# A scratch tensor stored by pairs of classes, read back into spread partitions on one queue

## The chip, the cores and the metric

The kernel runs on one core of a Trainium2 chip. A core has five engines with queues of their own: TensorE (PE, matrix products), VectorE (DVE), ScalarE (ACT), GpSimd (POOL) and SyncE (SP), which here only issues DMAs. SyncE's DMAs go through the queue that the profile calls q1 (hardware_dynamic), GpSimd's through q0 (software_dynamic). Both feed the same 16 DMA engines.

The metric is the time of one execution on the device, in microseconds (us). The kernel before takes 406.85 us, the median of three runs from 404.64 to 407.57. The profile comes from one more execution.

## The reference

Two layers follow each other. Here `x` is 8 x 5696 x 128 and `h` is 5696 x 128.

```python
Yf = np.fft.rfft(x, n=2*S, axis=1) * np.fft.rfft(h, n=2*S, axis=0)[None]   # long convolution
x  = np.fft.irfft(Yf, n=2*S, axis=1)[:, :S, :]
X  = np.fft.rfft(x, axis=1)                     # spectral mixing, first 64 modes only
Y[:, :64] = einsum('bmd,mde->bme', X[:, :64], w_r + 1j*w_i)
u  = x + np.fft.irfft(Y, n=S, axis=1)
out = u + np.maximum(u @ w_ch, 0.0)
```

## The kernel before

The sequence of 5696 positions is written as 89 x 64. A Fourier step over the 89 gives 90 frequency *classes* (`NK`), and the step over the 64 (`J`) is done class by class. The batch of 8 is taken in four groups of two (`NP` = 4, index `g_`). Every operation is recorded by a small planner, the `Recorder`, which derives each wait from named tokens that an operation reads, writes or must come after. Engines run their lists in the order of recording. The diff lies in three places, and the order of the work around them is this.

**Ticks.** A group runs through 23 ticks (`tick`, `NT` = 23) of up to four classes. A tick's matmuls transform four classes of both batch elements. VectorE multiplies with the spectrum of `h` (`products`, tensors U, Hs), two more matmuls per element turn the result back over the 64 positions, and ScalarE writes it in float16 to a small ring of buffers (Zs and Zt, lines 569 to 571). Such a buffer holds, on 128 partitions (real and imaginary part of 64 positions), four classes of 2 x 128 values. SyncE writes it to the scratch tensor `zscr` in DRAM (line 573): class after class, in each 128 rows of 256 values, so that every packet has 512 B. The same buffers feed matmuls that collect the 64 modes for the second layer. While the fourth group runs, GpSimd loads what comes later, in the table `early` by tick: the weights W, the table S4 in two parts (`load_s4`), and at tick 21 the first blocks of Z. The first block waits for the Z writes of ticks 0 to 14 of that group (`SLACK`).

**The passage.** After the last tick come 128 short matmuls of the modes with W, the transposes of their result Y, and in between the first work of the output stage (`u_z` with `alone`).

**Output stage.** It needs Z the other way round: for a position p within the 64, all classes on partitions. A *block* is one group's Z for 16 positions (`ZB`), 16 blocks in all. `load_zt` reads a block into one of five tiles: 180 rows (90 classes, real and imaginary), 8 KB each, the first 128 rows in part a on partitions 0 to 127, the other 52 in part b on partitions 32 to 83. Partitions 0 to 31 of part b are set to zero by GpSimd (line 477), since the matmul with part b covers partitions 0 to 83. Blocks 0 to 4 are read by GpSimd, the other 11 by SyncE, which also writes the output. A block's tile is loaded again when the block is used up: line 762, for the block five places on. `u_tile` makes 8 positions of one batch element: one matmul that adds the second layer (`u_c`, tables IBs, C), and for each position two matmuls with 89 columns, parts a and b of the block against parts a and b of S4. ScalarE or VectorE writes the result to UT. `o_tile` multiplies UT with `w_ch` and the identity (WI), ScalarE takes the ReLU into R, VectorE adds into O, and SyncE writes 512 KB for every pair of them. In group 0 only `u_tile` runs; from group 1 on the `o_tile`s of the group before are mixed in.

The reads of blocks 0 to 4 are recorded with two calls in `early` and two behind the ticks:

```python
NT - 2: lambda: (load_zt(0, "gpsimd", SLACK), load_ib(), load_zt(1, "gpsimd"), load_zt(2, "gpsimd"))}
...
load_wi()
load_zt(3, "gpsimd")
load_zt(4, "gpsimd")
```

All these tiles lie over tensors of the earlier stages. `zt_old` names the tokens whose readers must be done before a tile is first written; for block 4 they are the tables M and G.

Of the kernel before, what the change touches and what calls it, by code (L numbers as in the profile page):

```python
# [4 lines left out]
P = 128  # L5
F16 = mybir.dt.float16
# [117 lines left out]
def bass_long_conv_fft__then__afno_spectral_mix_kernel(nc, x, h, moe_w_r, moe_w_i, moe_w_ch, out):  # L124
# [31 lines left out]
    pos = J * qq[None, :] + pp[:, None]  # L156
    ang = 2.0 * np.pi * kk[:, None, None] * pos[None] / L
    s4 = np.stack([back[:, None, None] * np.cos(ang), -back[:, None, None] * np.sin(ang)], axis=0)
    RB, PB = 2 * NK - P, 32
    rows = s4.transpose(1, 0, 2, 3).reshape(2 * NK, S)  # L160
    s4t = np.zeros((P, 2 * S))
    s4t[:, 0:S] = rows[0:P]
    s4t[PB:PB + RB, S:2 * S] = rows[P:2 * NK]
    tt = np.arange(S)
    am = 2.0 * np.pi * np.outer(tt, np.arange(M)) / S
    modes = np.concatenate([np.cos(am), -np.sin(am)], axis=1)
# [75 lines left out]
    xt = at("XT", B * XTW, F16, a_g + GW * 2 + 2048 * (NZX - NZ))  # L242
    assert GW * 2 + 2048 * (NZX - NZ) + B * XTW * 2 <= HW * 2

    ZB = 16
    NC = 5
    ZP = ZB * 2 * D
    a_h2, a_xt = a_h + HW * 2, a_x + 4 * S + 2 * B * P
    a_as1, a_m2 = a_as + 2 * S, a_m + 4 * S
    zt_off = [(a_h, a_h2), (a_as1, a_as1 + 2 * ZP), (a_h + 2 * ZP, a_h2 + 2 * ZP), (a_as1 + 4 * ZP, a_as1 + 6 * ZP),  # L250
              (a_m2, a_g)]
    assert 2 * S + 8 * ZP <= AW * 2
    zt = [[at(f"ZT{i}{'ab'[p_]}", ZP, F16, zt_off[i][p_]) for p_ in range(2)] for i in range(NC)]
    ib_sb = at("IBs", S, F16, a_m)
    s4_sb = [at("S4a", S, F16, a_m + 2 * S), at("S4b", S, F16, a_as)]
    assert 4 * S + 2 * ZP + 4 * P + 2048 <= 2 * MW
    wi_sb = at("WI", 2 * P, F16, a_m2 + 2 * ZP)
    u_off = [a_x, a_x + 2 * S, a_st, a_st + 2 * S]
    u_sb = [at(f"UT{i}", S, F16, u_off[i]) for i in range(4)]
    o_big = [a_h + 4 * ZP, a_h2 + 4 * ZP, a_st + 4 * S] + [a_g + 2 * ZP + 4096 * i for i in range(2)] + \  # L260
            [a_xt + 4096 * i for i in range(2)]
    o_off = [a_h + 4 * ZP + 4096, a_h2 + 4 * ZP + 4096, a_m2 + 2 * ZP + 4 * P]
    NO8, NO = len(o_big), len(o_off)
# [18 lines left out]
        return bass.AP(ps, p0 * 4096 + bank * 512 + off, [[4096, n]] + [list(d) for d in dims])  # L282

    R = Recorder(nc)
    for name, n in (("c", 16), ("x", 26), ("z", 8), ("w", 16), ("t", 10), ("s", 8), ("o", 12), ("p", 16), ("q", 10)):
        R.ring(name, n)

    def bank(i):
# [175 lines left out]
    WT = [("w", i) for i in range(4)]  # L464
    ZY = [("zs", i, b) for i in range(NZL, NZX) for b in range(2)]
    ZX = [("zs", i, b) for i in range(NZ, NZL) for b in range(2)]
    zt_old = [(H_ALL, H_ALL), (AST, AST), (H_ALL, H_ALL), (AST, AST), (M_ALL[3:6], G_ALL)]

    def load_zt(i, eng="sync", more=()):
        g_, c_ = divmod(i, J // ZB)  # L470
        for part, (p0, r0, n) in enumerate(((0, 0, P), (PB, P, RB))):
            old = once(("zt", i % NC, part), zt_old[i % NC][part])
            if more:
                old = list(old) + list(more)
            if old and part:
                z32 = zt[i][1][0:PB, :].bitcast(U32)
                R.add("gpsimd", lambda e: e.memset(z32, 0), (), [("zt0", i)], after=old)  # L477
            dma(eng, bass.AP(zt[i % NC][part], p0 * ZP, [[ZP, n], [1, ZP]]),
                bass.AP(zs, (g_ * 2 * NK + r0) * J * 256 + c_ * ZB * 256, [[J * 256, n], [1, ZP]]),
                "q" if eng == "gpsimd" else "t", [("zd", g_, s_) for s_ in range(NT)], [("zt", i % NC, part)], after=old)  # L480

    def load_ib():
        dma("gpsimd", ib_sb[:, :], c_ib.ap(), "p", (), [("ib",)], after=M_ALL[0:2] + pace)

    def load_s4(part):
        n = PB + RB if part else P
        dma("gpsimd", s4_sb[part][0:n, :], bass.AP(c_s4, part * S, [[2 * S, n], [1, S]]), "p", (),
            [("s4", part)], after=pace + (AST if part else M_ALL[1:4]))

    V, A = "vector", "scalar"  # L490
    border = {NT - 1: [(0, 2, V)], NT: [(1, 0, V), (2, 2, A)], NT + 1: [(3, 0, V), (4, 2, A)], NT + 2: [(5, 0, V), (6, 2, V)]}
    early = {0: lambda: load_id(), 1: lambda: load_w(0), 3: lambda: load_w(1), 6: lambda: load_w(2), 8: lambda: load_w(3),
             12: lambda: load_s4(1), 16: lambda: load_s4(0),
             NT - 2: lambda: (load_zt(0, "gpsimd", SLACK), load_ib(), load_zt(1, "gpsimd"), load_zt(2, "gpsimd"))}
# [42 lines left out]
    def tick(g_, t):  # L537
        if g_ + 1 < NP:
            for i in range(2 * XC):
                if t == XPLACE[g_ > 0][i]:  # L540
                    x_place(i, x_st[i], xtok(i))
        with_h = with_h_at(g_, t)
        if t < NT:
            sl = XSLOT[0] if with_h else XSLOT[(t + (g_ == 0)) % 2]
            for i, k in enumerate(ticks[t]):
                for r in range(2):
                    for b in range(2):
                        col = k * 3 * J + (J if r == 0 else 0) + b * J
                        mm(pv(sl + b, i * D, [[1, D]]),
                           ap(m_sb, MW, J * b, J, col, [[1, P]]),  # L550
                           ap(a_sb, AW, J * b, J, (2 * k + r) * D, [[1, D]]), r == 0, r == 1,
                           AST + mtok(k), [bank(sl + b)])
            products(g_, t, sl)
        if t in border and g_ + 1 < NP:
            for j, sl, e in border[t]:
                a_tile(j, [sl], e)
        if g_ + 1 < NP and t % 2 == 0 and 0 < t <= 4 * XC:
            i = t // 2 - 1
            x_load(g_ + 1, i, x_st[i], xtok(i), [("u", t % NU)] + AST)
        if LC <= t < NT + LC:  # L560
# [12 lines left out]
            dma("sync", bass.AP(zs, zo, [[256, P], [P * 256, n], [1, 256]]),  # L573
                bass.AP(z_s[zi], 0, [[1024, P], [256, n], [1, 256]]), "z",
                [("zs", zi, 0), ("zs", zi, 1)], [("zd", g_, s_)])
        if LM <= t < NT + LM:
            s_ = t - LM
            zi = s_ % NZS[g_]
            if s_ == 0:
                mm(pv(MB, 0, [[1, 2 * P]]), m_sb[ZR:P, 0:P], ap(f1_sb, 2 * NK, ZR, P - ZR, 0, [[0, 2], [1, P]]), True, False, [("f1",)] + mtok(0), [bank(MB)])  # L580
            for i, k in enumerate(ticks[s_]):
                for b in range(2):
                    if k % 2:
                        o, off, n, sl = pv(MB, b * P, [[1, P]]), (k + 1) // 2 * P, P, (k + 1) // 2
                    else:
                        ms, off = even[k]
                        n, sl = 2 * len(ms), 0
                        dims = [[M, 2]] if len(ms) == 1 else [[ms[1] - ms[0], 2], [M, 2]]
                        o = pv(MB, b * P + ms[0], dims)
                    mm(o, z_s[zi][:, i * 256 + b * P:i * 256 + b * P + P], g_sb[:, off:off + n],  # L590
                       False, k == NK - 1 and b == 1, [("g", sl // GP), ("zs", zi, b)], [bank(MB)])
        if with_h:
            filter_tick(t + LH, [2, 3])
# [26 lines left out]
                    dma("gpsimd", dst, src_, ring, (), [tok], after=[("as", j)])  # L620


    load_wi()
    load_zt(3, "gpsimd")
    load_zt(4, "gpsimd")

    LSLOT = [4, 6, 0, 2]
    NCH = J // ZB
# [3 lines left out]
    def u_z(i, b, half, alone=False):  # L632
        g_, c_ = divmod(i, NCH)
        t = turns("l", LSLOT)
        z = zt[i % NC]
        for hb in range(2):
            if alone:
                mm(pv(t + hb, 0, [[1, 4 * NQ]]), f1_sb[ZR:P, 0:P], ap(f1_sb, 2 * NK, ZR, P - ZR, 0, [[0, 2], [1, 2 * NQ]]),
                   True, False, [("f1",)], [bank(t + hb)])
            else:  # L640
                u_c(i, b, half, t, hb, True)
            for pl in range(4):
                for ri in range(2):
                    pz = half * 8 + hb * 4 + pl
                    so = (c_ * ZB + pz) * NQ
                    n = (P, PB + RB)[ri]
                    mm(pv(t + hb, pl * NQ, [[1, NQ]]), z[ri][0:n, pz * 256 + b * P:pz * 256 + b * P + P], s4_sb[ri][0:n, so:so + NQ],
                       False, not alone and pl == 3 and ri == 1, [("zt", i % NC, ri), ("zt0", i % NC), ("s4", ri)], [bank(t + hb)])
        if alone:
            ahead[(i, b, half)] = t  # L650
        return t
# [149 lines left out]
```

## Time and profile before

| | |
|---|---|
| three runs | 407.57, 406.85, 404.64 us |
| the profiled execution | 409.74 us, of which its span is 407.7 us |
| mean granted clock of TensorE | 0.977 of full speed |
| TensorE busy | 376.7 us, 92% of the span |
| VectorE / ScalarE busy | 311.8 us (76%) / 296.4 us (73%) |
| GpSimd busy | 81.4 us (20%) |
| ticks of group 3 | about 229 to 272 us |
| passage | 272 to 291 us |
| output stage | 291 to 407.7 us |
| SyncE's queue (q1) | 62379 packets, 67.73 MB, 48.1% of the time of 16 engines |
| GpSimd's queue (q0) | 24288 packets, 37.31 MB, 43.0% |
| Z writes (zscr from Zs and Zt) | 88 of 256 KB and 4 of 128 KB |
| last Z write, 128 KB | 15.8 us from issue to landing |

Tensors go by the program's names: ZT0a is part a of the tile that holds blocks 0, 5, 10 and 15, ZT4b is part b of the tile of blocks 4, 9 and 14. The helper lines 312 (matmul), 300 and 302 (ScalarE), 304 and 306 (VectorE) and 309 (DMA) stand for many places, so rows are told apart by their tensors. A chain is followed back from the last instruction: at each step to what released it. In a table of waits, the first name is the one that waited.

### The profile page before, as it was taken

Reading aid. Unit: us, or ns where it says so; the run is one execution under the profiler, and the core shown is the slowest. Engines: PE = TensorE matmul, PEld = TensorE weight load, DVE = VectorE, ACT = ScalarE, POOL = GpSimd, SP = SyncE. Lnnn points to the kernel's source line nnn. Section 1 sums busy time; section 2 is a strip of 40 time slices with the busy share of each in tenths; the row PEclk is TensorE's granted clock in tenths of the full one; section 3 lists DMA queues with packets and bytes.
Section 4 is the critical chain, followed back from the end, with each engine's and each line's share of the span. In section 5 each row is a group of like instructions: output and inputs, shape, how many; then the busy total and the mean of one; then the engine's idle time right before and its main releaser. Section 6 shows DMA issues by size and latency. Waiting matters only on the chain.

```text
span 407.7 us, 12527 instructions
## 1 busy us (share of the span) xinstructions
PE 376.7 (92%) x5398; PEld 286.7 (70%) x5398; DVE 311.8 (76%) x341; ACT 296.4 (73%) x477; POOL 81.4 (20%) x133
## 2 busy tenths in 40 slices
PE   7979899998999988899989899997978999999994
PEld 7978666656756657656658666665767889888873
DVE  6878789997899997889997888850324677777876
ACT  1458599987978977788878888960434777777775
POOL 8300022210823202723304011039100000000000
PEclk9999999999999999999999999995798999999999
DMA  8997379995989993989985499999998999999869
GB/s 159 194 320 271 101 162 280 274 278 159 138 137 218 251 233 80 141 154 207 245 224 95 48 311 346 285 274 394 417 390 340 314 350 420 406 419 390 347 251 357
DMA packets 86720, 105.81 MB, mean 260 GB/s; under 512 B 22494, under 2 KB 72286, under 8 KB 82846
## 3 DMA queue, kind: packets, MB, share of 16 engines
q1 hardware_dynamic: 62379, 67.73, 48.1%
q0 software_dynamic: 24288, 37.31, 43.0%
q8 instruction: 42, 0.69, 0.7%
q14 instruction: 11, 0.09, 0.1%
HBM read 72.49 MB, written 51.12 MB: 303 GB/s over the span
## 4 chain that ended last, share of the span: by engine, by line
PE 56%; DMA 14%; DVE 11%; ACT 9%; POOL 6%; issue 2%; SPq 0%; DVEq 0%; POOLq 0%
PE ps L312 56%; DVE U L528 5%; DMA ZT4b<-zscr 5%; DVE As L306 5%; DMA Xr<-in_x_dram 4%; ACT As L302 4%; DMA zscr<-Zt 3%; POOL Xr L309 2%; DMA Hs<-Hs 2%; ACT Xs L300 2%; ACT R L735 1%; ACT UT L300 1%; ACT Zt L300 1%; DVE Xin L348 1%; POOL ZT1b L477 0%
## 5 line engine op out<-in xcount | busy, mean ns | idle before, releaser
L528 DVE TENSOR_TENSOR U<-Xs,Hs 128x2048 f16<-128x2048 f16 x70 | 82.7, 1190 | 20.2 <-ACT Xs L300 20.0
L312 PE MATMUL ps<-U,Wc 128*128 128x512 f16 (+1 forms) x368 | 93.6, 377 | 1.9 <-DVE U L528 1.9
L300 ACT CAST Zs<-ps 128x512 f16<-128x512 f32 (+1 forms) x142 | 75.7, 592 | 9.4 <-PE ps L312 9.4
L300 ACT CAST Xs<-ps 128x1024 f16<-128x1024 f32 x70 | 69.4, 996 | 15.6 <-PE ps L312 14.6
L736 DVE TENSOR_TENSOR O<-ps,R 128x512 f32<-128x512 f32 x81 | 52.5, 685 | 20.4 <-ACT R L735 12.0
L735 ACT ACTIVATE R<-ps 128x512 f32<-128x512 f32 x96 | 50.9, 572 | 18.8 <-PE ps L312 18.4
L306 DVE TENSOR_SCALAR As<-ps 128x720 f16<-128x720 f32 x68 | 57.6, 900 | 9.1 <-PE ps L312 8.5
L312 PE MATMUL ps<-As,M 64*128 64x128 f16 x1440 | 55.8, 217 | 5.1 <-ACT Xs L300 2.0
L312 PE MATMUL ps<-F,Xin 128*128 128x180 f16 x512 | 53.5, 249 | 7.0 <-DVE As L306 2.8
L312 PEld LDWEIGHTS ps<-F,Xin 128*128 128x128 f16 x512 | 44.6, 155 | 14.5 <-DVE As L306 4.1
L302 ACT ACTIVATE As<-ps 128x720 f16<-128x720 f32 x60 | 46.3, 785 | 10.6 <-PE ps L312 9.7
L312 PE MATMUL ps<-WI,UT 128*128 128x256 f16 x360 | 52.3, 280 | 0.5 <-DVE O L736 0.4
L312 PEld LDWEIGHTS ps<-As,M 64*128 64x128 f16 x1440 | 40.7, 94 | 15.1 <-DVE U L528 3.2
L312 PEld LDWEIGHTS ps<-U,Wc 128*128 128x128 f16 x368 | 29.1, 98 | 31.6 <-DVE U L528 2.4
L528 DVE TENSOR_TENSOR U<-ps,Hs 128x2048 f16<-128x2048 f32 x22 | 50.2, 2283 | 0.8 <-DMA Hs<-Hs 0.8
L309 POOL DMA_DIRECT2D Xt<-in_x_dram x48 | 25.5, 536 | 109.7 <-PE ps L312 94.7
L300 ACT CAST UT<-ps 128x712 f16<-128x712 f32 x40 | 30.0, 752 | 20.7 <-PE ps L312 19.7
L312 PEld LDWEIGHTS ps<-WI,UT 128*128 128x128 f16 x360 | 39.4, 152 | 4.3 <-issue 1.9
L312 PE MATMUL ps<-IBs,C 128*128 128x356 f16 x128 | 40.6, 327 | 0.6
L312 PEld LDWEIGHTS ps<-G,Zs 128*128 128x128 f16 x556 | 28.1, 96 | 14.9
L304 DVE CAST UT<-ps 128x712 f16<-128x712 f32 x24 | 21.4, 891 | 17.0 <-PE ps L312 17.0
L312 PE MATMUL ps<-G,Zs 128*128 128x128 f16 (+2 forms) x556 | 34.3, 192 | 0.0
(84 smaller groups left out, 497.0 us busy)
## 6 DMA issues: line engine op xcount, KB each, us to landing
out_dram<-O SPq DMA_DIRECT2D x39, 512.0 KB, 8.3
zscr<-Zs SPq DMA_DIRECT2D x68, 256.0 KB, 6.2
Xt<-in_x_dram POOLq DMA_DIRECT2D x24, 320.0 KB, 6.9
zscr<-Zt SPq DMA_DIRECT2D x20, 256.0 KB, 6.9
W<-wscr POOLq DMA_DIRECT2D x4, 1024.0 KB, 8.5
M<-cM POOLq DMA_DIRECT2D x5, 720.0 KB, 20.4
ZT0a<-zscr SPq DMA_DIRECT2D x3, 1024.0 KB, 9.9
Hs<-Hs SPq DMA_DIRECT2D x44, 64.0 KB, 5.9
```

What stands on the lines that cost most here:

```text
L300: R.add(e, lambda h_: h_.copy(dst, src), reads, writes, after=after)
L302: R.add(e, lambda h_: h_.activation(dst, src, COPY, scale=scale), reads, writes, after=after)
L304: R.add(e, lambda h_: h_.tensor_copy(dst, src), reads, writes, after=after)
L306: R.add(e, lambda h_: h_.tensor_scalar_mul(dst, src, scale), reads, writes, after=after)
L309: R.add(eng, lambda h_: h_.dma_start(dst, src), reads, writes, ring=ring, after=after)
L312: R.add("tensor", lambda h_: h_.matmul(o, l, r, start=st, stop=sp), reads, writes)
L348: R.add("vector", lambda e: e.tensor_copy(bass.AP(x_sb, i * XN * XS, [[XW, NQ], [XS, XN], [1, D]]), bass.AP(src, 0, [[XB, NQ], [D, XN], [1 ...
L528: R.add("vector", lambda e: e.tensor_tensor(uv, src, hv, MULT), bk + [("h", t, 0), ("h", t, 1, 0), ("h", t, 1, J)], [("u", i)])
L735: R.add("scalar", lambda e: e.activation(rv, src_r, RELU), bk, [("r", i % NR)], after=once(("r", i % NR), G_ALL + XTT + [("y", 0), ("y", 1 ...
L736: R.add("vector", lambda e: e.tensor_tensor(ov, src_u, rv, ADD), bk + [("r", i % NR)], [key + (h_,)], after=once(key, old))
```

## The change

Three things are done.

1. **Z's scratch by pairs of classes.** Row p of two neighbouring classes is stored together, 512 values. A buffer of four classes is written as two pairs, with packets of 1 KB.
2. **A block's rows spread.** The real and imaginary part of a pair of classes are two rows of 16 KB in a block, 90 rows in all. Rows 0 to 63 go to the even partitions 0, 2, ... 126, rows 64 to 89 to partitions 1, 5, ... 101. The other 38 partitions are set to zero, once for each tile, by a memset of the whole tile before its first read (`clear_zt`). The two matmuls for a position now take the first and the second class of every pair, each over 128 partitions. The table S4 is laid out in the same way, with a memset of its own for each part.
3. **GpSimd issues all reads of Z.** The two DMAs of each of the 16 blocks are on GpSimd's queue. SyncE has only the output in that stage.

With this the tiles move: a block has one tile of 16 KB a partition in place of two parts of 8 KB. Tile 4 now lies at the start of G, which covers the first of the buffers Zt too, so its memset also comes after the readers of those (`G_ALL + ZX + ZY`); two output buffers change place. The memsets of tiles 1 and 0 are at ticks 14 and 17 of the last group, those of the others right ahead of their reads.

```diff
-    s4t[:, 0:S] = rows[0:P]
-    s4t[PB:PB + RB, S:2 * S] = rows[P:2 * NK]
+    s4t = s4.transpose(1, 0, 2, 3).reshape(NK // 2, 2, 2, S).transpose(0, 2, 1, 3).reshape(NK, 2 * S)
...
+    SPREAD = ((0, J, 0, 2), (J, NK - J, 1, 4))
...
-    zt_off = [(a_h, a_h2), (a_as1, a_as1 + 2 * ZP), (a_h + 2 * ZP, a_h2 + 2 * ZP), (a_as1 + 4 * ZP, a_as1 + 6 * ZP),
-              (a_m2, a_g)]
+    zt_off = [a_h, a_as1, a_h2, a_as1 + 4 * ZP, a_g]
...
-    zt_old = [(H_ALL, H_ALL), (AST, AST), (H_ALL, H_ALL), (AST, AST), (M_ALL[3:6], G_ALL)]
-
-    def load_zt(i, eng="sync", more=()):
+    zt_old = [H_ALL, AST, H_ALL, AST, G_ALL + ZX + ZY]
+
+    def load_zt(i, more=()):
         g_, c_ = divmod(i, J // ZB)
-        for part, (p0, r0, n) in enumerate(((0, 0, P), (PB, P, RB))):
...
+        old = list(once(("zt", i % NC), zt_old[i % NC])) + list(more)
+        for part, (r0, n, p0, st) in enumerate(SPREAD):
+            dma("gpsimd", bass.AP(zt[i % NC], p0 * 2 * ZP, [[st * 2 * ZP, n], [1, 2 * ZP]]),
+                bass.AP(zs, g_ * NK * P * 256 + r0 * J * 512 + c_ * ZB * 512, [[J * 512, n], [1, 2 * ZP]]),
+                "q", [("zd", g_, s_) for s_ in range(NT)] + [("zc", i % NC)], [("zt", i % NC, part)], after=old)
+
+    def clear_zt(i):
+        z32 = zt[i][:, :].bitcast(U32)
+        R.add("gpsimd", lambda e: e.memset(z32, 0), (), [("zc", i)], after=list(zt_old[i]) + pace)
...
     def load_s4(part):
...
+        s32 = s4_sb[part][:, :].bitcast(U32)
+        R.add("gpsimd", lambda e: e.memset(s32, 0), (), [("s4z", part)], after=old)
+        for h_, (r0, n, p0, st) in enumerate(SPREAD):
...
-             NT - 2: lambda: (load_zt(0, "gpsimd", SLACK), load_ib(), load_zt(1, "gpsimd"), load_zt(2, "gpsimd"))}
+             14: lambda: clear_zt(1),
+             17: lambda: clear_zt(0),
+             NT - 2: lambda: (load_zt(0, SLACK), load_ib(), load_zt(1), clear_zt(2), load_zt(2))}
...
-            dma("sync", bass.AP(zs, zo, [[256, P], [P * 256, n], [1, 256]]),
-                bass.AP(z_s[zi], 0, [[1024, P], [256, n], [1, 256]]), "z",
+            dma("sync", bass.AP(zs, zo, [[512, P], [P * 512, n // 2], [1, 512]]),
+                bass.AP(z_s[zi], 0, [[1024, P], [512, n // 2], [1, 512]]), "z",
...
     load_wi()
-    load_zt(3, "gpsimd")
-    load_zt(4, "gpsimd")
+    clear_zt(3)
+    load_zt(3)
+    clear_zt(4)
+    load_zt(4)
...
-                    mm(pv(t + hb, pl * NQ, [[1, NQ]]), z[ri][0:n, pz * 256 + b * P:pz * 256 + b * P + P], s4_sb[ri][0:n, so:so + NQ],
+                    zo = pz * 512 + ri * 256 + b * P
+                    mm(pv(t + hb, pl * NQ, [[1, NQ]]), z[:, zo:zo + P], s4_sb[ri][:, so:so + NQ],
```

More of the change, by code (lines that the diff above doesn't have):

```diff
@@ L158, in bass_long_conv_fft__then__afno_spectral_mix_kernel @@
     s4 = np.stack([back[:, None, None] * np.cos(ang), -back[:, None, None] * np.sin(ang)], axis=0)
-    RB, PB = 2 * NK - P, 32
-    rows = s4.transpose(1, 0, 2, 3).reshape(2 * NK, S)
-    s4t = np.zeros((P, 2 * S))
-    s4t[:, 0:S] = rows[0:P]
-    s4t[PB:PB + RB, S:2 * S] = rows[P:2 * NK]
+    s4t = s4.transpose(1, 0, 2, 3).reshape(NK // 2, 2, 2, S).transpose(0, 2, 1, 3).reshape(NK, 2 * S)
     tt = np.arange(S)
@@ L249, in bass_long_conv_fft__then__afno_spectral_mix_kernel @@
     a_as1, a_m2 = a_as + 2 * S, a_m + 4 * S
-    zt_off = [(a_h, a_h2), (a_as1, a_as1 + 2 * ZP), (a_h + 2 * ZP, a_h2 + 2 * ZP), (a_as1 + 4 * ZP, a_as1 + 6 * ZP),
-              (a_m2, a_g)]
+    zt_off = [a_h, a_as1, a_h2, a_as1 + 4 * ZP, a_g]
     assert 2 * S + 8 * ZP <= AW * 2
-    zt = [[at(f"ZT{i}{'ab'[p_]}", ZP, F16, zt_off[i][p_]) for p_ in range(2)] for i in range(NC)]
+    zt = [at(f"ZT{i}", 2 * ZP, F16, zt_off[i]) for i in range(NC)]
     ib_sb = at("IBs", S, F16, a_m)
@@ L259, in bass_long_conv_fft__then__afno_spectral_mix_kernel @@
     u_sb = [at(f"UT{i}", S, F16, u_off[i]) for i in range(4)]
-    o_big = [a_h + 4 * ZP, a_h2 + 4 * ZP, a_st + 4 * S] + [a_g + 2 * ZP + 4096 * i for i in range(2)] + \
+    o_big = [a_h + 4 * ZP, a_h2 + 4 * ZP, a_st + 4 * S] + [a_m2 + 4096 * i for i in range(2)] + \
             [a_xt + 4096 * i for i in range(2)]
@@ L284, in bass_long_conv_fft__then__afno_spectral_mix_kernel @@
     R = Recorder(nc)
-    for name, n in (("c", 16), ("x", 26), ("z", 8), ("w", 16), ("t", 10), ("s", 8), ("o", 12), ("p", 16), ("q", 10)):
+    for name, n in (("c", 16), ("x", 26), ("z", 8), ("w", 16), ("t", 10), ("s", 8), ("o", 12), ("p", 16), ("q", 12)):
         R.ring(name, n)
@@ L466, in bass_long_conv_fft__then__afno_spectral_mix_kernel @@
     ZX = [("zs", i, b) for i in range(NZ, NZL) for b in range(2)]
-    zt_old = [(H_ALL, H_ALL), (AST, AST), (H_ALL, H_ALL), (AST, AST), (M_ALL[3:6], G_ALL)]
-    def load_zt(i, eng="sync", more=()):
+    zt_old = [H_ALL, AST, H_ALL, AST, G_ALL + ZX + ZY]
+    def load_zt(i, more=()):
         g_, c_ = divmod(i, J // ZB)
-        for part, (p0, r0, n) in enumerate(((0, 0, P), (PB, P, RB))):
[L472 to L480, printed above, removed]
+        old = list(once(("zt", i % NC), zt_old[i % NC])) + list(more)
[6 more added lines that the diff above has]
+        R.add("gpsimd", lambda e: e.memset(z32, 0), (), [("zc", i)], after=list(zt_old[i]) + pace)
     def load_ib():
@@ L485, in load_s4 @@
     def load_s4(part):
-        n = PB + RB if part else P
-        dma("gpsimd", s4_sb[part][0:n, :], bass.AP(c_s4, part * S, [[2 * S, n], [1, S]]), "p", (),
-            [("s4", part)], after=pace + (AST if part else M_ALL[1:4]))
+        old = pace + (AST if part else M_ALL[1:4])
+        s32 = s4_sb[part][:, :].bitcast(U32)
+        R.add("gpsimd", lambda e: e.memset(s32, 0), (), [("s4z", part)], after=old)
+        for h_, (r0, n, p0, st) in enumerate(SPREAD):
+            dma("gpsimd", bass.AP(s4_sb[part], p0 * S, [[st * S, n], [1, S]]), bass.AP(c_s4, (r0 * 2 + part) * S, [[2 * S, n], [1, S]]),
+                "p", [("s4z", part)], [("s4", part, 0, h_)], after=old)
     V, A = "vector", "scalar"
@@ L620, in bass_long_conv_fft__then__afno_spectral_mix_kernel @@
                     dma("gpsimd", dst, src_, ring, (), [tok], after=[("as", j)])
+    pace[:] = []
     load_wi()
-    load_zt(3, "gpsimd")
-    load_zt(4, "gpsimd")
+    clear_zt(3)
+    load_zt(3)
+    clear_zt(4)
+    load_zt(4)
     LSLOT = [4, 6, 0, 2]
@@ L645, in u_z @@
                     so = (c_ * ZB + pz) * NQ
-                    n = (P, PB + RB)[ri]
-                    mm(pv(t + hb, pl * NQ, [[1, NQ]]), z[ri][0:n, pz * 256 + b * P:pz * 256 + b * P + P], s4_sb[ri][0:n, so:so + NQ],
-                       False, not alone and pl == 3 and ri == 1, [("zt", i % NC, ri), ("zt0", i % NC), ("s4", ri)], [bank(t + hb)])
+                    zo = pz * 512 + ri * 256 + b * P
+                    mm(pv(t + hb, pl * NQ, [[1, NQ]]), z[:, zo:zo + P], s4_sb[ri][:, so:so + NQ],
+                       False, not alone and pl == 3 and ri == 1, [("zc", i % NC), ("zt", i % NC, 0), ("zt", i % NC, 1), ("s4", ri, 0, 0), ("s4", ri, 0, 1), ("s4z", ri)], [bank(t + hb)])
         if alone:
@@ L700, in bass_long_conv_fft__then__afno_spectral_mix_kernel @@
     o_cur = [0]
-    o8_old = [H_ALL] * 2 + [U_ALL] + [G_ALL + ZX] * 2 + [WT] * 2
+    o8_old = [H_ALL] * 2 + [U_ALL] + [M_ALL[3:6]] * 2 + [WT] * 2
     o_old = [H_ALL] * 2 + [M_ALL[5:6]]
```

## The prediction

> **What bounds the kernel now.** I read the chain of work that ended last, then who waited for whom on TensorE, then the granted clock in steps of 1 us, then the DMA queues in windows. After the loads at the start the chain is nearly all engine work, and TensorE is busy 100% of the time from 240 to 270 us and 99% from 320 to 380. The exception is the passage from the ticks to the output stage (start, duration, work):
>
> ```profile
> 260.02 10.88 DMA zscr<-Zt
> ...
> 271.95 1.81 POOL ZT0b L477
> ...
> 284.73 1.74 POOL ZT4b L477
> 286.47 20.44 DMA ZT4b<-zscr
> 306.91 0.04 issue
> 306.95 13.93 PE ps L312 x182
> ```
>
> A write of Z, landed at 270.9, releases GpSimd's first read of Z. Five blocks follow with a memset in each, and the last part of the fifth takes 20.4 us to land. TensorE's waits there (total, times, longest):
>
> ```profile
> PE ps L312 <- DMA ZT4b<-zscr: 2.4, 1, 2.4
> PE ps L312 <- DMA ZT0b<-zscr: 2.4, 1, 2.4
> PE ps L312 <- DMA ZT3b<-zscr: 0.7, 1, 0.7
> PE ps L312 <- DMA ZT4a<-zscr: 0.7, 1, 0.7
> ```
>
> That is 6.2 us of plain waiting. The clock adds to it (last three columns: granted clock, DMA share, GB/s):
>
> ```profile
> 276.00:277.00 1.00, 1.00 (x40) 1.00 (x37) 0.29 (x1) 0.00 (x0) 1.00 (x1) 0.55 0.83 287
> 289.00:290.00 1.00, 1.00 (x9) 0.62 (x8) 0.53 (x1) 0.78 (x2) 0.00 (x0) 0.63 0.99 418
> 306.00:307.00 1.00, 0.05 (x1) 0.05 (x2) 0.00 (x0) 0.00 (x0) 0.00 (x0) 0.91 0.96 401
> 310.00:311.00 1.00, 1.00 (x17) 0.93 (x15) 0.69 (x1) 0.18 (x2) 0.00 (x0) 0.89 0.79 336
> ```
>
> Between the first two rows the clock is 0.50, and again between the last two: about 276.55 to 289.63 and 306.91 to 310.11. The first drop comes before any wait for Z, under the 128 short matmuls on W, so it will stay.
>
> Why do blocks 3 and 4 come late? In the window 280 to 284 GpSimd's queue moves 1.66 MB in 4 us, 415 GB/s, with the engines to itself. In 300 to 306, while TensorE waits for block 4 on that queue, SyncE's queue has taken the engines:
>
> ```profile
> q0 software_dynamic: 182, 1.66, 97.6%
> ...
> q1 hardware_dynamic: 250, 1.75, 71.7%
> q0 software_dynamic: 98, 0.60, 23.7%
> ```
>
> (packets, MB, share; first row 280 to 284, the others 300 to 306). SyncE issues the reads of blocks 5, 6 and 7, not needed before 310, at 290.8, 294.7 and 298.7, and they pass block 4.
>
> **The change, part by part.**
>
> *Reads all on GpSimd.* Blocks 0 to 4 and the two small tables are 5 x 1.475 + 1.458 + 0.066 = 8.9 MB; with about 1 MB of Z writes still outstanding at 271.4 that is 9.9 MB. The rows of GB/s sum to 9.0 MB by 295 and 9.9 MB by 297; what landed until 306.9 was 13.7 MB, so 3.8 MB of later blocks had gone ahead. In one queue they can't. Block by block at the measured 410 GB/s: block 1 lands at about 285, block 2 at 289, block 3 at 293.
>
> Block 4 has a condition of its own. Its tile now lies over two of the buffers from which Z is written, so its memset waits for the very last Z write. That one was issued at 273.0 and took 15.8 us, so 288.8. The memset is 128x4096 words; the nearest row is
>
> ```profile
> L477 POOL MEMSET ZT0b<- x1: 1824/1824/1824, 271.9 to 271.9; 32x2048 uint32 x1
> ```
>
> so 0.89 ns a word and 3.65 us, if the number of partitions doesn't count. The block's reads are issued at 292.5 and 293.0 and land 6.7 to 7.1 us later by the rows of block 0: 299.6. TensorE needs it after blocks 1 to 3 at 3.93 us each (290.80, 294.7, 298.7 in the SyncE reads they release): from block 1 at 289.5 (below) that is 301.3. All three late waits go, 3.8 us, and with them the half-speed 3.2 us that follow: 1.6 us. **5.4 us.**
>
> *Block 0.* GpSimd's memset between its two parts goes, so the second part is issued 0.53 us behind the first, not 2.3. Lower bound of the first issue: VectorE's product of tick 21 ends at 269.9; upper: 271.4 as now. With 7 us to land, block 0 is there between 277.5 and 279; I take 278.3 against 280.84, 2.5 us earlier. TensorE then runs at half clock until 289.63, so 2.5 us are worth half: **1.3 us**, block 1 starting at 289.5. If the clock came back one of its steps of 3.4 us earlier it would be 1.6 us more; that is an end of the range.
>
> *GpSimd's added work before the passage.* Two memsets of 2848 words (2.53 us each) and two of 4096 (3.65 each), two more DMA issues (0.53). From 253.5: 2.53 + 1.07 + 3.65 ends at 260.7; from 260.9 the same again ends at 268.2. The earliest start of block 0 is 269.9, so 1.7 us of idle GpSimd hide it: zero. VectorE's operations that ran beside a memset kept their time (the 128x512 cast of Y, inside the memset at 275.3, took 0.69 us; the 712-wide cast alone takes 0.90), but none of these has two inputs in SBUF as the products have. Bounds: zero to all 12.4 us added to VectorE; I take zero, the nearest row. [...]
>
> *Z written by pairs.* 22,528 fewer packets. In 276 to 280 SyncE's queue spends 48.2% of 64 engine-us on 1159 packets of 512 B, 26.6 ns each; at the rate of the long rows 512 B would take 19.3. So 7.3 ns a packet, some 10 us of all 16 engines over the span, 2.5 of it in the last group. TensorE is busy throughout there; the one wait that it could end is VectorE's 0.8 us for a mirrored half of H. Zero to 0.8; I take zero.
>
> *Matmuls.* Same number; 128 rows for 84 costs nothing (204 and 203 ns in the rows of ZT0b and ZT0a).
>
> *What is late next.* The DMA engines. From 271.4: 5 us for tables and last Z writes, 23.6 MB of Z at 424 GB/s = 55.7, 23.3 MB of output at 406 GB/s (the window 366 to 376) = 57.4. That ends at 389.5 at the earliest, against a last matmul at 399.4 - 6.7 = 392.7. It still fits: zero, with up to 2 us of waiting for output buffers as the bound.
>
> **Sum:** 5.4 + 1.3 = 6.7 us off the profiled execution's span of 407.7: 401.0, and its time 409.7 becomes 403.0. That execution lies 2.9 us above the median of 406.85, so I predict 400.1.
>
> **Rivals.**
>
> *Slower: the spread reads move fewer bytes per us.* Nothing in the trace reads 64 rows into every second partition. The DMA bound above decides: at 340 GB/s the Z reads need 69.4 us, the engines are done at 403.2, and with the last output's landing the gain is gone; at 300 GB/s they need 78.7, end at 412.5 and the span at about 415. Time: **414**. For it: SyncE's queue is already at 97 to 102% from 320 to 360. Against: the packets get longer (16 KB rows), and long rows have the best rate in the trace. [...] The 415 GB/s above come from rows in adjacent partitions.
>
> *No change that can be measured* (1% here): the last Z write lands after 293 instead of 288.8, since it shares the engines with rows twice as long. Block 4's memset and reads follow it, the wait for block 4 and its clock drop stay, and only 1.3 + 0.7 + about 1 remain: **404**.
>
> *Slower: the memsets.* If 128 partitions took twice the time of 32, or the products blocked them, the first pair would end at 266.9 and the second at 280.4: block 0 is issued 9 us late. The 3.8 us of late waits still go, so 5 us stay: **412**.
>
> **Chances.** Forecast 0.55, slow reads 0.23, no change 0.15, memsets 0.07. The range: down to 397 (6.7 + 1.6 + 0.8, and a little), up to 414, which leaves out 5% below and half of the slow reads above. Faster by over 1% 0.56, within 1% 0.15, slower 0.29. One per cent is about what this kernel's runs can tell from nothing (404.6 to 407.6 before).
>
> **What would show it.** Right: no TensorE wait for blocks 3 and 4 and a clock of 1.00 from about 290 to the end; block 0's first matmul at 278 to 279; GpSimd's queue over 400 GB/s while alone. Wrong: reads under 340 GB/s, TensorE waits for Z after 320, VectorE waiting for output buffers, products longer than 1.23 us beside a memset, or block 4's memset starting after 293.

## The result, and the profile after

The changed kernel takes **424.91 us** (median of four runs, 424.48 to 427.03), against 406.26 for the kernel before in the same four rounds. The ratio is 1.047, 95% interval 1.0425 to 1.0516: 18.6 us slower, where 6.7 us faster was forecast and the range ended at 414. The profiled execution took 427.03 us, of which its span is 425.2. Ratios and intervals, here and below, are taken from fast runs in the same rounds, so they can differ by a few tenths of a per cent from the quotient of the medians beside them.

The chain of work that ended last, after the change (start, duration, work):

```profile
269.13 1.24 DVE U L528
...
270.66 1.05 POOL ZT L305 x2
...
277.62 17.83 DMA ZT<-zscr
...
296.48 3.51 POOL ZT L475
...
301.01 6.53 DMA ZT<-zscr
...
307.58 13.91 PE ps L308 x183
...
323.58 26.76 DMA out_dram<-Os
```

Down to the first read it goes as predicted: VectorE's last product, then GpSimd's two DMAs of block 0 at once. Then the second DMA of block 2 takes 17.8 us to land, block 4's memset (the row at 296.48) begins 7.7 us later than worked out (288.8), and TensorE starts on block 4 at 307.58, where it was 306.95 before. The whole gain of the passage is gone, but only 0.6 us are lost by then. The rest lies behind it: from block 4 to the end it is 117.6 us, where it was 100.8. And there the chain holds what it did not hold before, a write of the output that takes 26.8 us to land.

TensorE's waits after the change (total, times, longest):

```profile
PE ps L308 <- DVE Os L739: 6.9, 1, 6.9
PE ps L308 <- DMA ZT<-zscr: 6.4, 4, 2.8
PE ps L308 <- DVE O L739: 4.9, 2, 4.5
```

The middle row answers to the four rows of before: 6.2 us of waits for Z have become 6.4. The other two are new, but for one wait of 0.4 us for O that the kernel before has too. TensorE waits there for VectorE to add into O and Os, and VectorE's own waits say why (same columns):

```profile
DVE Os L739 <- DMA out_dram<-Os: 8.8, 1, 8.8
...
DVE O L739 <- DMA out_dram<-O: 4.9, 1, 4.9
```

VectorE can't write an output buffer whose last content is still on its way to DRAM. The longer of the two waits stands before one short addition:

```profile
350.47 0.28 DVE L739 TENSOR_TENSOR Os<-ps,R 64x128 f32<-64x128 f32 x1 [8.80 <-DMA out_dram<-Os]
```

Most of a batch element goes out in writes of 512 KB from seven buffers (O). Its last rows go out in two short writes, of 256 and of 32 KB, from a ring of only three smaller buffers (Os, `NO` in the kernel). So the buffer of one element's 256 KB is wanted again for the last rows of the next element. Here that write was issued at 323.58, the buffer was wanted at 341.7, and the write landed at 350.3.

The windows of TensorE, granted clock and DMA (last three columns: clock, DMA share, GB/s):

```profile
284.00:288.00 4.00, 4.00 (x36) 2.78 (x35) 0.42 (x1) 0.60 (x1) 0.09 (x1) 0.50 1.06 288
288.00:292.00 4.00, 4.00 (x39) 2.93 (x38) 1.69 (x2) 1.41 (x2) 0.00 (x0) 0.58 0.94 284
292.00:296.00 4.00, 3.75 (x72) 3.13 (x69) 1.01 (x2) 2.26 (x3) 0.00 (x0) 1.00 0.88 293
296.00:300.00 4.00, 3.45 (x64) 2.88 (x62) 1.56 (x2) 1.50 (x2) 3.50 (x1) 1.00 0.33 94
...
330.00:340.00 10.00, 5.52 (x74) 4.63 (x72) 4.11 (x7) 4.34 (x7) 1.05 (x2) 0.96 1.02 384
340.00:350.00 10.00, 3.96 (x43) 2.97 (x41) 0.69 (x1) 2.10 (x4) 0.00 (x0) 0.67 0.89 326
350.00:360.00 10.00, 9.11 (x97) 7.78 (x98) 5.92 (x9) 4.88 (x8) 1.05 (x2) 0.69 0.88 329
```

Three things are to be seen. From 284 to 296 the engines are busy and move 284 to 293 GB/s, where the kernel before moved 415 in 280 to 284. Of the window 284 to 288 the queue of the reads has the greater part:

```profile
q0 software_dynamic: 130, 1.04, 94.8%
```

From 296 to 300, under block 4's memset, the engines are two thirds idle, since nothing can be read. And between 330 and 360 TensorE loses what the kernel loses. Its busy time by the granted clock is 5.3, 2.7 and 6.3 us of 10 in these windows, so 15.7 of the 16.8 us are missing here: in plain waits, and because the clock is 0.50 behind the first long wait (about 339 to 342) and from the middle of the second on (346 to 356, in steps of 1 us).

How long do the outputs take? From issue to landing, of those issued between 313 and 335, before and after (KB each, median us):

```profile
out_dram<-O SPq DMA_DIRECT2D x10, 512.0 KB, 8.3
```

```profile
out_dram<-O SPq DMA_DIRECT2D x9, 512.0 KB, 23.3
```

In that stretch after the change GpSimd's queue has 77.9% of the engines and SyncE's 23.4%. With 23 to 27 us on each write, the seven large buffers and the three small ones run out.

So three suspects stand: the spread rows move slowly; the one queue of reads starves the output; block 4's memset stops the reads and then lets them all go at once. They were taken apart one at a time, and then in pairs.

### The profile page after: what moved, and what is told of

It reads as the page before. It is cut to its first block, busy times and chain, and to the rows that moved or that the text cites. A ratio compares the mean times of both kernels' runs of the same rounds, so it can differ in the third digit from the quotient of the medians.

```text
span 425.2 us, 12544 instructions
## 1 busy us (share of the span) xinstructions
PE 381.4 (90%) x5398; PEld 288.5 (68%) x5398; DVE 312.2 (73%) x341; ACT 296.9 (70%) x477; POOL 107.6 (25%) x159
## 4 chain that ended last, share of the span: by engine, by line
PE 48%; DMA 19%; DVE 13%; ACT 9%; POOL 5%; issue 4%; DVEq 0%; POOLq 0%
PE ps L308 48%; DVE U L528 6%; DMA out_dram<-Os 6%; DMA ZT<-zscr 6%; ACT As L298 5%; DVE As L302 4%; DMA Xr<-in_x_dram 4%; DMA Xt<-in_x_dram 3%; ACT Xs L296 2%; POOL Xr L305 2%; POOL ZT L475 2%; ACT R L738 1%; DVE Hs L300 1%; POOL ZT L305 1%; ACT UT L296 1%
## 5 line engine op out<-in xcount | busy, mean ns | idle before, releaser
L308 PE MATMUL ps<-S4a,ZT 128*128 128x89 f16 x512 | 61.2, 212 | 8.1 <-DMA ZT<-zscr 6.4
L308 PE MATMUL ps<-WI,UT 128*128 128x256 f16 x360 | 54.9, 289 | 11.9 <-DVE Os L739 6.9
L308 PE MATMUL ps<-S4b,ZT 128*128 128x89 f16 x512 | 61.4, 212 | 0.0
L308 PEld LDWEIGHTS ps<-S4a,ZT 128*128 128x128 f16 x512 | 48.5, 103 | 10.0 <-DMA ZT<-zscr 7.6
L308 PEld LDWEIGHTS ps<-S4b,ZT 128*128 128x128 f16 x512 | 47.0, 103 | 8.7 <-issue 1.8
```

Of the source, the lines that this page charges most:

```text
L308: R.add("tensor", lambda h_: h_.matmul(o, l, r, start=st, stop=sp), reads, writes)
```

## Experiments: which part of the change

**SyncE reads blocks 5 to 15 again**, in the new layout.

```diff
-            dma("gpsimd", bass.AP(zt[i % NC], ...
+            dma("gpsimd" if i < NC else "sync", bass.AP(zt[i % NC], ...
```

> The changed kernel with one part undone: blocks 5 to 15 of Z are read by SyncE again, in line with the output; blocks 0 to 4 stay on GpSimd, the spread rows and the scratch by pairs stay. Theory Q (the queues): the loss of 17 us after 307 us comes from GpSimd's reads taking the DMA engines from the output writes, which then land 16 to 28 us after their issue and hold up VectorE. By it the waits of VectorE for out_dram (8.8 and 4.9 us) are gone and the time is 405 to 410 us, near the kernel before, since block 4 comes at 307 in both. Theory R (the rate): the spread rows move at about 300 GB/s in place of 424, on whichever queue; by it the DMA engines stay the bound and the time is 415 to 425 us, with TensorE waiting for Z after 320 us.

426.23 us against 409.67, ratio 1.0406 (1.0329 to 1.0484). The intervals of this and of the full change overlap: undoing the third part gives back little or nothing. TensorE's waits:

```profile
PE ps L308 <- DMA ZT<-zscr: 19.5, 4, 9.5
...
PE ps L308 <- DVE Os L739: 1.5, 1, 1.5
```

The stalls for the output are nearly gone, and TensorE waits 19.5 us for Z instead. This is the picture of the theory of the rate, 1 us beyond its range. There isn't enough transfer rate for both; the order of the queues only decides who goes without.

**The old layout with all reads on GpSimd**, the third part alone.

```diff
-                load_zt(i + NC)
+                load_zt(i + NC, "gpsimd")
```

> The kernel before with one part of the change alone: GpSimd issues all reads of Z, in the old layout (128 rows and 52 rows of 8 KB). Theory Q: GpSimd's queue starves the output here too; output writes land 15 us or more after their issue, VectorE waits for them, the time is 412 to 425 us. Theory R: the old rows keep their 415 to 425 GB/s, the waits for blocks 3 and 4 are gone and the output isn't held up: 399 to 403 us.

408.55 against 409.67, ratio 0.9972 (0.9937 to 1.0008): nothing that can be told, and outside the ranges of both theories. In its profile the waits for blocks 3 and 4 are gone, as the prediction's main step has it. Waits for the output stand in their place, and the wait for block 0 is as before (2.4 us there):

```profile
PE ps L312 <- DVE Os L736: 3.2, 3, 2.3
...
PE ps L312 <- DMA ZT0b<-zscr: 2.5, 1, 2.5
```

The engines move 391 to 418 GB/s from 284 to 312 here. Outputs issued between 313 and 340 land in 13.4 us, while the engines move 411 GB/s in all (before, in 313 to 335, it was 8.3 us at 320 GB/s), and VectorE waits 5.3 us for them, all of it for the three small buffers. So the one queue has a price of its own, but the price is of the size of its gain.

**The old layout with only blocks 5 to 7 moved to GpSimd**, so that nothing passes block 4 and SyncE still reads the rest.

```diff
+                load_zt(i + NC, "gpsimd" if i + NC < 8 else "sync")
```

> The kernel before with only the reads of blocks 5, 6 and 7 moved to GpSimd's queue, behind blocks 0 to 4; the old layout, blocks 8 to 15 on SyncE as before. It asks whether the wait for blocks 3 and 4 was worth what the prediction said, when neither the spread rows nor reads beside the output are there. If the step was right: no TensorE wait for blocks 3 and 4, 5.4 us less, 400 to 403 us on the scale of 406.9 (ratio 0.985 to 0.99). If the gain is given back as with all reads on GpSimd: ratio 0.995 to 1.005, with VectorE waiting for the output.

405.54 against 407.15, ratio 0.9956 (0.9917 to 0.9996). Here the step is seen in its pure form. Of the waits for Z there is one left:

```profile
PE ps L312 <- DMA ZT0b<-zscr: 0.9, 1, 0.9
```

The span is 401.9 us, 5.8 below that of before, and the step was put at 5.4. But the times say 1.6. Most of the difference lies in which executions were profiled: that of before is 2.9 us over its median (406.85), that of this kernel (403.87) 1.7 us under its own, together 4.6. So neither expectation is met whole: the ratio is that of a gain given back (0.995 to 1.005), but VectorE's waits for the output, which were to be the reason, are only 0.2 us.

**The same, and the zero rows of the first three tiles written during the ticks**, so that GpSimd does not put a memset between the two parts of block 0.

```diff
+             ... 17: lambda: clear_zt(1), 18: lambda: (clear_zt(0), clear_zt(2)),
```

> As the run with blocks 5 to 7 on GpSimd, and the memsets of the first three tiles moved to ticks 17 and 18, so that block 0's second part is issued 0.5 us behind its first. By the prediction's step on block 0: another 1.3 us, 399 to 402 us on the scale of 406.9, TensorE's wait for ZT0b under 1 us. If the 15 us to land are set by the engines and not by the issue: the wait for ZT0b stays over 2 us and the time is that of the other run.

404.74 against 407.15, ratio 0.9972 (0.9933 to 1.001). The wait for block 0 is 0.2 us in its profile, but TensorE waits 1.3 us for Os there, and the interval overlaps the last one: this step's 1.3 us are not resolved.

**The 90 rows on neighbouring partitions**, 0 to 89, all else as in the change.

```diff
-    SPREAD = ((0, J, 0, 2), (J, NK - J, 1, 4))
+    SPREAD = ((0, J, 0, 1), (J, NK - J, J, 1))
```

> The changed kernel with the 90 rows on partitions 0 to 89, without zero rows between (the other partitions stay zero behind them); all else as changed. [...] Theory Q alone: within 1% of 425 us.

458.36 against 409.67, ratio 1.1158 (1.1068 to 1.1247). Waits for Z 17.4 us, for Os 15.2, for O 10.5. The partitions alone, with the same bytes in the same rows on the same queue, move the time by some 7% (1.1158 against 1.047). The chosen spread is far better than none, and still not good.

**Block 4's memset freed**: in group 3 six Z buffers in place of eight, so that none lies under tile 4. The first read of Z still waits for ticks 0 to 14.

```diff
-    NZS = [NZ] + [NZX] * (NP - 2) + [8]
+    NZS = [NZ] + [NZX] * (NP - 2) + [6]
```

> The changed kernel with the last group's Z written through six buffers in place of eight, so that block 4's memset has no Z write of that group to wait for (in the changed kernel it waits until 296.5 us, 23.5 us after the last write's issue). If that chain and the burst of five blocks behind it are a main part of the loss: block 4's wait of 2.8 us and the clock drop behind it go, and the time falls to 417 to 421 us. If the rate of the spread rows is what counts: the reads only wait elsewhere, 422 to 426 us.

427.19 against 407.15, ratio 1.0515 (1.0471 to 1.056): no gain at all. The stop at 296 is gone from the profile (DMA share 1.00 from 292 to 300), but what the engines do in that time is slow:

```profile
292.00:300.00 8.00, 6.37 (x124) 5.48 (x121) 1.80 (x2) 3.54 (x5) 1.05 (x2) 1.00 1.00 277
300.00:306.00 6.00, 3.42 (x39) 2.73 (x37) 0.90 (x1) 0.84 (x2) 1.05 (x2) 0.74 1.04 273
306.00:312.00 6.00, 5.42 (x89) 4.78 (x88) 2.49 (x3) 2.64 (x4) 1.05 (x2) 0.98 0.93 251
```

Neither the queue nor the stop explains the loss while the reads run below 300 GB/s. What makes them slow?

## Experiments: why the spread reads are slow

Three kernels do nothing but transfers, of bytes of the right sizes; none of the reference's computation is in them.

**Reads of blocks with nothing beside them.** Four blocks in each of four layouts, by GpSimd and by SyncE, and then five blocks with five outputs beside them.

> The disputed cost by itself; nothing is computed, and the output is only written with zeros in part. Four blocks of 1.47 MB are read back to back from x, in four layouts one after the other (Half: 128 and 52 rows of 8 KB; Spread: 64 and 26 rows of 16 KB on every second and every fourth partition; Next: the same rows on partitions 0 to 89; Cut: Spread with each row in four pieces of 4 KB), first all on GpSimd's queue, then all on SyncE's. Then, for Half, Spread and Cut, GpSimd issues five blocks while SyncE writes five outputs of 512 KB. Theory R: Half at 400 GB/s or more, Spread at 270 to 330 on both queues. Theory Q: Half and Spread alike, over 400, when alone; beside five blocks of Spread the outputs land 15 to 25 us after their issue, beside Cut clearly earlier (the engines would take turns by packets of 16 KB against 4 KB), beside Half in between.

Windows inside each phase (last column GB/s): on GpSimd's queue the old layout, the changed one, rows 0 to 89 adjacent, the changed one cut into 4 KB; then the first three on SyncE's.

```profile
13.00:26.00 13.00, 0.00 (x0) 1.12 (x3) 1.00 0.95 401
31.00:48.00 17.00, 0.00 (x0) 0.67 (x2) 1.00 0.94 301
53.00:80.00 27.00, 0.00 (x0) 0.67 (x2) 1.00 0.93 197
85.00:101.00 16.00, 0.00 (x0) 0.63 (x2) 1.00 0.97 318
106.00:118.50 12.50, 0.00 (x0) 0.00 (x0) 1.00 0.95 402
123.50:140.00 16.50, 0.00 (x0) 0.00 (x0) 1.00 0.93 311
145.00:172.00 27.00, 0.00 (x0) 0.00 (x0) 1.00 0.93 196
```

The engines are busy 0.93 or more of the time in all of them. The layout costs a quarter of the rate, on either queue. The fourth layout tells nothing of the rows' length: its phase has 511 packets on GpSimd's queue, the uncut one 512, for the same 5.90 MB, so the trace doesn't show the cut into 4 KB. Beside five reads, the five outputs of 512 KB land (median) in 11.5 us for the old layout, 16.4 for the changed one and 15.8 for that meant to be in pieces.

**Shapes of one DMA at a time in steady flow.**

> Reads alone again, nothing computed and the output not written: some 6.3 MB of x each in nine shapes on GpSimd's queue, one shape after the other. Full16 and Full8: 128 adjacent partitions, rows of 16 KB (64 KB apart in DRAM) or 8 KB (32 KB apart). Even16 and Even8: the same rows into the 64 even partitions. Quart16: the 26 rows on every fourth partition from 1. Mid8: the old 52 rows on partitions 32 to 83. Low16: partitions 0 to 31. Duo16: 32 rows to partitions 0 to 31 and 32 to 64 to 95 in turn. Spr16: the spread pair of the changed kernel. Three theories of the 301 GB/s. Long rows far apart in DRAM are slow: Full16 near 300, Full8 over 400. [...] The 26 rows are slow (13 engines, two rows each): Even16 over 380, Quart16 under 250, and Mid8, the old counterpart, over 300. [...]

Sixty-four rows of 16 KB on the even partitions, and 32 rows on partitions 0 to 31:

```profile
47.00:60.00 13.00, 0.00 (x0) 1.58 (x3) 1.00 0.99 421
...
89.00:114.00 25.00, 0.00 (x0) 4.43 (x9) 1.00 1.01 206
```

One DMA of 1.05 MB follows another every 2.46 us on the even partitions, 426 GB/s, and every 2.48 us (424 GB/s) with all 128 partitions in rows of 8 KB. So the row length, the pitch and the stride of two cost nothing, and the 64 rows of a block are not at fault. The 26 rows on 1, 5, ... 101 follow each other every 2.09 us, 204 GB/s. They are the fault. (Two shapes with short DMAs were bound by their landing of 4.6 and 4.9 us with three in flight, and tell nothing. The 26 rows land in 6.0 us and come near that bound, so the next run has five in flight.)

**The 26 rows, with five DMAs in flight.** They lie on 1, 5, ... 101 (step 4, as in the change), 33, 35, ... 83, then 1, 3, ... 51, then 64 to 89; after these come whole blocks with the first and with the second.

> Reads alone, nothing computed and the output not written. The 26 rows of 16 KB by themselves on four sets of partitions: ByFour, every fourth from 1 (the changed kernel's); ByTwo, every second from 33 to 83; ByTwoLow, every second from 1 to 51; Adj, 64 to 89. Then whole blocks: SprFour is the changed kernel's pair, SprTwo has its second part ByTwo. [...] Rival: 13 engines with two long rows each are slow as such; by it ByTwo stays at 205 and SprTwo at 300.

```profile
15.00:34.00 19.00, 0.00 (x0) 4.55 (x10) 1.00 0.82 222
46.00:58.00 12.00, 0.00 (x0) 4.92 (x10) 1.00 0.81 343
68.00:94.00 26.00, 0.00 (x0) 4.98 (x10) 1.00 0.82 165
109.00:135.00 26.00, 0.00 (x0) 4.98 (x10) 1.00 0.81 165
150.00:168.00 18.00, 0.00 (x0) 0.00 (x0) 1.00 0.93 311
176.00:190.00 14.00, 0.00 (x0) 0.17 (x1) 1.00 0.94 400
```

Two losses are in the first four rows. The DMA share is 0.81 to 0.82 in all of them, where the 64 rows on the even partitions have 0.99. That is 13 of 16 engines, as if the 26 rows were shared out two to an engine: an estimate from the share, since no trace shows which engine takes which row. And at this one share the rate goes by the partitions: by the intervals between issues, 221, 351, 164 and 166 GB/s. So the rival, by which 33, 35, ... 83 would stay at 205, is refuted. With these partitions a whole block runs at 400 GB/s, the rate of the old layout (401).

Why some partitions are slow, no run shows. A stride of two gives 426 GB/s with 64 rows on 0, 2, ... 126, 351 with 26 rows on 33, 35, ... 83 and 164 on 1, 3, ... 51; neighbouring partitions give 424 on 0 to 127, 206 on 0 to 31, 196 or 197 to a whole block on 0 to 89 and 166 to the 26 rows on 64 to 89. So neither the stride nor the neighbourhood tells a slow set from a fast one. Which partitions are slow is measured, why is open.

## Experiments: the loss taken back step by step

**The change with the 26 rows on 33, 35, ... 83.**

```diff
-    SPREAD = ((0, J, 0, 2), (J, NK - J, 1, 4))
+    SPREAD = ((0, J, 0, 2), (J, NK - J, 33, 2))
```

> The changed kernel with one number pair changed: the 26 rows of a block (and of S4) go to partitions 33, 35, ... 83 in place of 1, 5, ... 101. All else as changed. If the rate of those 26 rows is the cause of the slowdown: reads over 380 GB/s, no TensorE wait for Z after 310 us, output waits as with all reads on GpSimd in the old layout (5 us of VectorE or less), time 400 to 409 us. If not: 420 us or more.

415.39 against 407.11, ratio 1.0205 (1.0171 to 1.0239). More than half of the loss goes with 26 partition numbers (the rows of S4 move along). It is less than was expected: 400 to 409 us. The last Z write now lands in 18.7 us (23.5 in the change), block 4's memset starts at 292.43, and TensorE waits 1.6 us for Z. What stays is the output: 1.9 us for O and 7.7 us for Os, after a write that took 23.6 us.

**The same, with blocks 8 to 15 read by SyncE.**

```diff
-            dma("gpsimd", bass.AP(zt[i % NC], ...
+            dma("gpsimd" if i < 8 else "sync", bass.AP(zt[i % NC], ...
```

> As the run with partitions 33 to 83, and blocks 8 to 15 read by SyncE; GpSimd keeps blocks 0 to 7. If the output's starvation by GpSimd's queue is what is left then: VectorE's waits for out_dram go and the time is 2 to 4 us below that run, 398 to 405 us. Otherwise the same within 1 us.

406.98 against 407.11, ratio 1.000 (0.9964 to 1.0035). That is 8.4 us below the run before it, where 2 to 4 were expected. Waits for Os 2.8 us, for Z 1.1. The new layout is no worse than the old one once its rows are well placed and the output shares a queue with its reads.

Why does the first of these two lose 2%, when the old layout with all reads on GpSimd loses nothing? Two causes were supposed: the stop before block 4, or that rows of 16 KB take turns with the output's packets of 4 KB (no trace shows turns). Each was to be taken away alone.

**Without the stop** (26 rows on 33, ..., six Z buffers in group 3, all reads on GpSimd).

> The changed kernel with the 26 rows on partitions 33, 35, ... 83, and in group 3 six Z buffers in place of eight, so that block 4's memset no longer waits for the last Z write. Theory stop (the DMA engines lie half idle from 292 to 300 us behind block 4's memset, 1.6 MB less read, and the nine reads that follow at once hold up the first outputs): DMA share over 0.95 from 292 to 300, TensorE's waits for VectorE's Os and O fall from 9.6 us to under 4, time within 0.6% of before. Theory long rows (16 KB reads take turns with 4 KB output packets): outputs still land in 18 to 20 us, waits for Os and O stay at 7 us or more, time 1.5 to 2.5% over before.

409.39 against 407.15, ratio 1.0023 (0.9983 to 1.0063). The window 292 to 300 with the stop, and without it:

```profile
292.00:300.00 8.00, 8.00 (x155) 7.13 (x153) 2.70 (x3) 4.10 (x6) 7.09 (x8) 1.00 0.53 196
```

```profile
292.00:300.00 8.00, 8.00 (x152) 7.14 (x150) 3.13 (x4) 3.93 (x6) 2.28 (x5) 1.00 1.01 416
```

In these 8 us 1.56 MB move with the stop and 3.33 without; the 1.77 MB that are missing are 4.3 us of all engines at 416 GB/s. TensorE doesn't notice at the time (8.00 of 8.00 busy in both). The bill comes later: from 320 to 350 TensorE is busy 20.4 of 30 us with the stop, 23.2 without. (In the single window 330 to 340 it is 3.33 against 6.15, but without the stop the long wait also begins earlier, before 330.) The waits for Z and for O are gone, but for 0.4 us. One part of the expectation failed: the wait for Os is still 6.4 us, in one piece, where under 4 was expected for all. So taking the stop away, with the two Z buffers that it costs, takes the 2% away, but not that one long wait. For it are left the one queue of reads, the long rows on it, and the ring of three small buffers, which was the same in all runs.

**With the rows in 4 KB pieces** (26 rows on 33, ..., the stop left in, all reads on GpSimd).

```diff
-            dma("gpsimd", bass.AP(zt[i % NC], p0 * 2 * ZP, [[st * 2 * ZP, n], [1, 2 * ZP]]),
+            dma("gpsimd", bass.AP(zt[i % NC], p0 * 2 * ZP, [[st * 2 * ZP, n], [2 * ZP // 4, 4], [1, 2 * ZP // 4]]),
```

> The changed kernel with the 26 rows on partitions 33, 35, ... 83, and each row of 16 KB read as four pieces of 4 KB in the same DMA, all on GpSimd. Theory long rows: the outputs land in under 15 us at 315 to 350 us, TensorE's waits for Os and O fall under 4 us, time within 0.6% of before. Theory stop: the stop at 292 to 300 us stays, and so do the waits (7 us or more) and the time, 1.5 to 2.5% over before.

413.81 against 407.15, ratio 1.0145 (1.0054 to 1.0235). The waits for Os and O are 6.4 and 2.4 us. But the cut doesn't show in the trace. GpSimd's queue (packets, MB, share) with the rows whole, and with the rows in pieces:

```profile
q0 software_dynamic: 25216, 53.16, 52.3%
```

```profile
q0 software_dynamic: 25216, 53.16, 52.4%
```

The packets are as many as before, so by the trace this is the run with 33, 35, ... once more, and the two intervals overlap. It says nothing of long rows. The run without the stop does: it has the rows of 16 KB whole and lies at 1.0023, at most 1.0063, so they are not what costs the 2%. Whether they have a part in the wait of 6.4 us stays open.

**All three mended**: 33, 35, ..., no stop, blocks 8 to 15 by SyncE.

> As e11, and blocks 8 to 15 read by SyncE. Theory stop: the time lost at 292 to 300 us is there in this order too, and taking it away gives back what waits for Os, O and ZT are left (4.3 us): 0.5 to 1% under before, 403 to 405. Theory long rows: the stop costs nothing here, since SyncE's reads come in their turn between outputs; time as with the stop, within 0.4% of before.

404.25 against 407.15, ratio 0.9937 (0.9909 to 0.9965). This is a version faster than both kernels, by 0.6% against the one before, and the only one here whose interval lies clearly below 1. From the run without the stop it differs only by the queue of blocks 8 to 15, so the one queue of reads is what the 0.9% between them goes back to (1.0023 to 0.9937, intervals apart). Three short waits for Z and the output are left in its output stage, all behind 350 us: 0.5 us for Z, 0.4 for O, and the longest:

```profile
PE ps L308 <- DVE Os L739: 1.8, 1, 1.8
```

From 284 to 350 the engines now move 392 GB/s or more in windows of 6 to 10 us, and TensorE has no wait for Z. A fourth small buffer for Os was not tried, in this kernel or any other.

The ladder, in ratios to before: 1.047 as changed; 1.0205 with the 26 rows moved; 1.0023 with the stop gone too; 0.9937 with SyncE's reads back. The order matters: made alone in the changed kernel, freeing block 4 gave 1.0515, and reads on SyncE (there from block 5 on) 1.0406.

## Why the prediction was wrong

The step that failed first is the rate in **Reads all on GpSimd**: "block by block at the measured 410 GB/s". That number came from rows on adjacent partitions, as the rival on the spread reads itself says. Measured: 284 to 293 GB/s in the kernel, 301 to 311 alone. The 64 rows do have the rate that was assumed (426); the 26 rows have half of it (221). So block 1 landed at about 290, block 2 at 295.5 and block 3 at 300.8, where the prediction had 285, 289 and 293.

From that one term the others follow. **Block 4**: its last Z write was to land at 288.8, with the 15.8 us of before. It shares the engines with slow reads, took 23.5 us and landed at 296.4. (The profile names TensorE as what released the memset at 296.48, for which it waits too; with six buffers the memset has no such wait.) The memset itself took 3.51 us where 3.65 was estimated, and the reads 6.5 where 6.7 to 7.1 was taken. So the chain was right link by link, and 7.6 us late in its first one. **Block 0**: issued at 270.66, inside the bounds, its two DMAs together as foretold, but its second DMA took 9.1 us to land where 7 was taken, its first matmul came at 280.37, not at 278.3, and half speed held until 291.3 as before until 289.7 (13.65 us at 0.50 in both, the next drop 3.41 us in both). Of 1.3 us nothing is to be seen.

**What is late next** failed in a way of its own. It put the engines' end at 389.5 and the wait for output buffers at 2 us at most. Measured: 11.8 us of waits (6.9 and 4.9), and in the 16.8 us lost there is also the clock at 0.50 behind them. The sum over the whole stage asked whether the engines finish in time. It did not ask whether an output lands before its buffer is wanted again, and it did not see the ring of three small buffers, on which the longer wait fell. In the old layout, where the engines do finish in time, moving the queue alone brings 5.3 us of such waits on VectorE and 3.6 on TensorE.

**The rivals.** "The spread reads move fewer bytes per us" is what happened; it had a chance of 0.23 and 414 us, which is its sum at 300 GB/s. Its mechanism was right, its rate was close, and its price was too small by 11 us, because it priced only the engines' end. The loss fell instead between 330 and 360, behind outputs that share the engines with reads and take 23.3 us to land (issued from 313 to 335; 8.3 before). Nor was the rate its only condition: with 33, 35, ... the engines move 386 to 425 GB/s in all windows from 284 to 330 but the one of the stop, and still 2% were lost. That is the rival "no change", the late last Z write: its point (after 293) was passed in the changed kernel (296.4) and nearly reached with 33, 35, ... (292.3). What the stop behind it costs was measured there as 1.8% (1.0205 to 1.0023), where 404 us, a gain, had been written beside it. It too left out that reads held back come all at once later. The memsets as a rival are refuted: VectorE's products beside a memset of 128x4096 words kept 1.22 to 1.23 us.

**What was right.** Blocks 3 and 4 came late because later blocks passed them; with these held back in the old layout the waits go and the span is 5.8 us shorter, for 5.4 forecast. Even so the sum was too good: it was made from one execution's waits, and the times of that kernel give 1.6 us. A forecast from the waits of one execution, which already stood 2.9 us over the median, can count that execution's bad luck as gain; the waits of the other executions were not traced, so this is argued, not shown. **Z by pairs** was costed at zero and gave zero: from 60 to 230 us SyncE's queue has 20,100 packets for 37,470 and its share falls from 38.8% to 32.8%, some 10 us of all 16 engines, but the fourth group's first ScalarE copy starts at 229.95 against 229.47. TensorE was busy 159.5 of these 170 us. (The 22,528 packets of the prediction leave out the four short writes; with them it is 23,040, and the term stays zero.) **Matmuls** over 128 rows for 84: 204 ns, as taken.

## What to carry to other kernels

Where a layout changes the partitions of a DMA, its rate has to be measured for just these partitions and this number of rows; the rate of another shape on the same queue is no estimate for it (here 164 to 351 GB/s for the same 26 rows). Where two streams share the engines, the sum of bytes over the stage tells only whether it can end in time. What stalled VectorE here was the landing time of the slower stream against the number of its buffers, most of all in the shortest ring (8.8 us for one write of 26.8 us, with three buffers). And a stop in one stream, free when it happened (TensorE busy 8.00 of 8.00 us), was paid when the held-back transfers came together (20.4 of 30 us busy, 23.2 without the stop). Mend the rate first: queue order and waits show their worth only when there is enough of it.

## What the runs showed that was not expected

Twenty-six rows of 16 KB read into SBUF go at 221 GB/s on partitions 1, 5, ... 101, at 351 on 33, 35, ... 83, at 164 on 1, 3, ... 51 and at 166 on 64 to 89, each time at a DMA share of 0.81 to 0.82, which is that of 13 of 16 engines; 64 rows on every second partition go at 426. Outputs that share the engines with reads on the other queue take 13.4 us to land, with 411 GB/s moved in all, where 8.3 did with all on one queue at 320 GB/s, and 23.3 us beside the changed kernel's reads. A packet of 1 KB in place of two of 512 B saved about 9.4 ns of one engine for each packet dropped, an estimate from the two shares of SyncE's queue between 60 and 230 us (10.2 us x 16 engines / 17,370 packets).
